# A spectral-mixing and GeGLU kernel on one core: soft threshold and half of the gates computed in place in PSUM, a pace for the background work in each stretch, and the inverse transform placed ahead of the last products

## The chip, the cores and the metric

The kernel runs on one core of one Trainium2 chip. The metric is the device time of one execution in microseconds (us), lower being better; the number compared is the median of several executions. The engines are named as the profile names them: PE (TensorE's matmuls), PEld (TensorE's weight loads), DVE (VectorE), ACT (ScalarE), POOL (GpSimd), SP (SyncE, which here only starts DMAs).

## What is computed

Everything works on x, 8192 rows of 448 numbers. Its layer norm goes into a spectral filter (branch A) and into a gated feed-forward network (branch B):

```python
D, F, NB, BS = 448, 1792, 4, 112
def A(x):                                   # x after the layer norm
    Xf = rfft2(x, axes=(1, 2))              # along the 8192 rows
    z = Xf.reshape(B, H, Wf, NB, BS)
    hr = relu(zr @ w1[0] - zi @ w1[1] + b1[0]); hi = relu(zi @ w1[0] + zr @ w1[1] + b1[1])
    or_ = hr @ w2[0] - hi @ w2[1] + b2[0];      oi_ = hi @ w2[0] + hr @ w2[1] + b2[1]
    or_ = sign(or_) * max(abs(or_) - 0.01, 0);  oi_ = sign(oi_) * max(abs(oi_) - 0.01, 0)
    return irfft2(or_ + 1j * oi_)
def Bf(x):
    return (gelu(x @ w_gate) * (x @ w_up)) @ w_down
xn = layernorm(x)
out = x + A(xn) * silu(Bf(xn))
```

The line with `sign` is the soft threshold. The factor `silu(Bf(xn))` is called the gate here. (Cut from the reference, which is evaluated in float32.)

## The kernel before

**Numbers in pairs.** TensorE is fed with float16. Each float32 operand is cut into a float16 head and a float16 rest (`hi`, `lo`), and a product becomes three matmuls: head by head, head by rest, rest by head. So most values that TensorE reads pass through one cast (ACT) and one subtraction (DVE or POOL).

**Branch B is the foreground.** Its products fill TensorE almost throughout. The 8192 rows come in 16 chunks of 512, and the hidden width of 1792 is done in two passes: pass 0 takes the first eight blocks of 128, pass 1 the last six. In `chunk`, the up and gate products of a chunk are built from seven smaller products per pair of blocks (`unit`: `a1` to `a7`), and the product with `w_down` is built from seven as well (`down2`, `prod2`). Between these, ACT computes the gelu, DVE multiplies by the up half (`glu`), and `sums` forms the sums and the head and rest pairs that the seven down products need. These sums are the tensors named `wt` in pass 1 and `u`, `gl` in pass 0; the pairs end in `h`, `left` and, again, `wt`.

`down2` holds two PSUM banks, x and y, out of the ring `BD`. A bank collects one product, DVE adds it to a running total in SBUF (`add2`, the tensor `left`), and the bank is used for the next product. Pass 0 stores the totals to HBM (`prt`); pass 1 loads them again (`pt_loads`), adds, and `ended2` turns the total into the gate: ACT takes tanh, DVE computes (tanh + 1) * total. The gate goes to HBM (`gsp`) or, once the inverse transform has begun (`state["direct"]`), straight into the output through `gate`.

**Branch A is the background.** It is woven between the products of the foreground in three phases. Phase 1 (`chunk1`, 16 chunks) normalizes x and does the first step of the transform (`stage1`); beside it the weights of branch B are scaled and split (`gu_comb`, `maxima`, `largest`, tensors `wst`, `wo`, `mxr`). Phase 2 (`phase2`, `group`) has 16 groups of frequencies by four channel blocks, 64 in all: second step of the transform, first layer with its relu (`layer1`), second layer, soft threshold, first step of the inverse transform (`stage3`). Phase 3 (`tiles3`, `gate_bank`) is the last step of the inverse transform, the multiplication by the gate and the sum with x, and writes the output. PSUM for the background comes out of `BF`; `BF` and `BD` share four banks (`Banks`), and a background request leaves one free unless the foreground already holds two.

**The soft threshold of a group.** The second layer's sum stands in a PSUM bank `b`. ACT writes relu(s * b - t) into the SBUF tensor `o`. A second piece goes into the SBUF tensor `va`: relu(-s * b - t) from ACT, or min(b + t', 0) from DVE, whichever engine is free earlier in the plan. The bank is given back. Then `o` becomes the difference of the two (DVE, or POOL where only a subtraction is left), and `halves` turns `o` into head and rest: ACT writes the head into `va`, DVE the rest.

**The plan.** No scheduler of the chip decides the order. The Python code itself keeps a clock for each engine (`Pace`) with estimated durations, and emits each instruction when the plan says that its inputs are there; the emitted order of each engine is then fixed. Semaphores hold back whatever is early on the chip. What steers it:

- `STEPS`, a table whose rows start at a planned time and hold: an allowance for DMA landings in us, how far an engine may be booked ahead before a background instruction is held, a factor on the planned durations, and a handicap for POOL. `Either` (the engine `B`) sends a subtraction or sum to DVE or to POOL, whichever ends earlier in the plan after the handicap; a negative one favours POOL.
- Due times of the background: phase 1 starts a chunk every 34 us (`DT`), phase 2 spreads its groups until `END2`, phase 3 its tiles until `END3`.
- `calm`, which lets a background instruction wait in the plan while foreground work is due on the engine.

All instructions are recorded by one helper, so every instruction of the profile stands on line 288 (290 in the changed kernel, which is two lines longer there). They are told apart by their tensors. In the order, a name like `bd_66` is one of the four shared PSUM banks (66 to 69), `by` and `bx` are the foreground's own banks, `th` the gate, `g` the gate loaded from HBM, `ms`, `fc`, `rowc` columns of factors.

The edited places are `STEPS` (line 43), `note` (150), `last_half` (1780), `ended2` (1797), the soft threshold in `group` (2311 to 2335), `END3` (2368), `phase2`, `phase3` (2462) and `first` (2785).

Of the kernel before, what the change touches and what calls it, by code (L numbers as in the profile page):

```python
# [11 lines left out]
F32 = mybir.dt.float32  # L12
# [10 lines left out]
NG = 16  # L23
CH = 4
# [18 lines left out]
STEPS = ((0, 2.75, 0.05, 0.97, 0.0), (15, 2.75, 0.05, 0.97, 0.0), (25, 2.75, 0.05, 1.0, 0.3), (35, 2.75, 0.05, 1.0, 0.3), (45, 2.75, 0.05, 1.07, 0.0), (55, 2.75, 0.05, 1.07, 0.0), (65, 2.75, 0.05, 0.97, 0.0), (75, 2.75, 0.05, 0.97, 0.0), (87, 2.75, 0.15, 1.01, 0.0), (100, 2.75, 0.15, 1.01, 0.0), (125, 2.5, 0.15, 1.04, 0.0), (150, 2.5, 0.15, 1.04, 0.0), (175, 2.5, 0.15, 1.04, 0.0), (200, 2.5, 0.15, 1.04, 0.0), (225, 3.0, 0.15, 0.98, 0.0), (250, 2.75, 0.05, 1.0, 0.0), (275, 2.75, 0.05, 1.0, 0.0), (300, 2.75, 0.05, 1.0, 0.0), (325, 2.5, 0.05, 1.02, 0.0), (350, 2.5, 0.05, 1.02, 0.0), (375, 2.5, 0.05, 1.04, -0.3), (400, 2.5, 0.05, 1.04, -0.3), (425, 2.5, 0.05, 1.04, -0.3), (450, 2.5, 0.05, 1.04, -0.3), (475, 2.5, 0.05, 1.04, -0.3), (500, 2.5, 0.05, 1.04, -0.3), (525, 2.5, 0.05, 1.04, -0.3), (550, 2.5, 0.05, 1.04, -0.3), (575, 3.5, 0.05, 1.0, 0.0), (600, 3.5, 0.05, 1.0, 0.0), (625, 3.5, 0.05, 1.04, 0.0), (650, 3.5, 0.05, 1.04, 0.0), (675, 3.5, 0.05, 1.04, 0.0), (700, 3.5, 0.05, 1.04, 0.0), (725, 2.75, 0.05, 1.0, 0.0), (750, 2.75, 0.05, 1.0, 0.0), (775, 3.0, 0.05, 1.0, -0.3), (800, 3.0, 0.05, 1.0, -0.3), (825, 3.0, 0.05, 1.0, -0.5), (850, 3.0, 0.05, 1.0, -0.5), (875, 3.0, 0.05, 1.0, -0.5), (900, 3.0, 0.05, 1.0, -0.5), (925, 2.75, 0.05, 1.06, 0.0), (950, 2.75, 0.05, 1.06, 0.0), (975, 2.75, 0.05, 1.06, 0.0), (1000, 2.75, 0.05, 1.06, 0.0), (1025, 2.75, 0.05, 1.06, 0.0), (1050, 2.75, 0.05, 1.06, 0.0), (1075, 2.75, 0.05, 1.06, 0.1), (1100, 2.75, 0.05, 1.06, 0.1), (1125, 2.75, 0.05, 1.02, 0.0), (1150, 2.75, 0.05, 1.02, 0.0), (1175, 1.75, 0.05, 1.025, 0.0), (1200, 1.75, 0.05, 1.025, 0.0), (1225, 1.75, 0.05, 1.055, 0.0), (1250, 1.75, 0.05, 1.055, 0.0), (1275, 1.75, 0.05, 1.025, -0.2), (1300, 1.75, 0.05, 1.025, -0.2), (1325, 1.75, 0.05, 1.025, -0.2), (1350, 1.75, 0.05, 1.025, -0.2), (1375, 1.75, 0.05, 1.025, -0.4), (1400, 1.75, 0.05, 1.025, -0.4), (1425, 2.25, 0.1, 1.025, -0.4), (1450, 2.25, 0.1, 1.025, -0.4), (1475, 2.25, 0.1, 1.025, -0.4), (1500, 2.25, 0.1, 1.025, -0.4), (1525, 2.25, 0.1, 1.025, -0.4), (1550, 2.25, 0.1, 1.025, -0.4), (1575, 1.75, 0.1, 1.025, -0.4), (1600, 1.75, 0.1, 1.025, -0.4), (1625, 1.75, 0.1, 1.025, -0.4), (1650, 1.75, 0.1, 1.025, -0.4), (1675, 2.75, 0.05, 0.94, 0.1), (1700, 2.75, 0.05, 0.94, 0.1), (1725, 2.75, 0.05, 0.94, 0.4))  # L43
# [15 lines left out]
class Pace:  # L59
# [496 lines left out]
def afno_geglu_kernel(ctx, tc, x, gu, raw, wd, mlp, b1, b2, c_m, c_mt, c_small, c_rows, out):  # L556
# [1222 lines left out]
    def last_half(i, qq, e, tf, a):  # L1779
# [13 lines left out]
        V.tensor_tensor(th, th, x4, op=ALU.add)  # L1793
        yield
        Q.dma_start(blk(ov[:, CH * i:CH * i + CH, :], *qq)[:, v], th)

    def ended2(p, i, qq, b, R, earlier=None):
# [19 lines left out]
        if i < NG - 1:  # L1817
            yield
            V.scalar_tensor_tensor(th, th, 1.0, q, op0=ALU.add, op1=ALU.mult)
            PT.put(q)  # L1820
            yield
            if i >= state["direct"]:
                yield from gate(i, qq, th)
                Q.dma_start(blk(ov[:, CH * i:CH * i + CH, :], *qq), th)
                TH.put(tf)
                return
            Q.dma_start(blk(chunk_of(gsp, i), *qq), th)
            TH.put(tf)
            EV["gn", i] = EV.get(("gn", i), 0) + 1
            if EV["gn", i] == 4:  # L1830
                done("gsp", i)
            return
# [8 lines left out]
        V.tensor_tensor(th, th, x4, op=ALU.add)  # L1841
# [407 lines left out]
    def group(g, n):  # L2249
# [579 lines left out]
```

## Time and profile before

| | before |
|---|---|
| median of 3 runs | 1739.8 us (1739.71 to 1740.24) |
| the profiled execution's own time | 1737.31 us |
| its span, first to last instruction | 1735.5 us |
| granted TensorE clock | 0.999 |
| PE busy | 1709.6 us of the span, 15654 matmuls |
| DVE, ACT, POOL busy | 1404.9, 1097.0, 937.6 us |
| bytes moved by DMA | 316.63 MB, 182 GB/s over the span |

How to read it. The profiled execution took 1737.31 us; 1735.5 us of that lie between its first and its last instruction, and the remaining 1.8 us around them. It is 2.5 us below the median of the three timed runs, so a gain is worked out against the profiled execution and then taken from the median. PE is busy 99% of the span. That figure counts a matmul as busy from its start to its modelled end, and consecutive ones overlap, so what can be gained without taking products away is only the time in which PE stands still, before, between and after the products. The idle column of the other engines is of interest only where PE waits for them.

### The profile page before, as it was taken

The page shows a single profiled execution, that of the slowest core. Times are in us where ns is not written, and L with a number is a line of the kernel's source. Part 1 is how long each engine was busy: PE and PEld are TensorE (multiplying, and loading weights), DVE is VectorE, ACT ScalarE, POOL GpSimd, SP SyncE. Part 2 cuts the span into 40 slices and gives each one's busy share as a digit, 9 for nine tenths or more (in the row PEclk, how much of TensorE's full clock was granted, in tenths as well). Part 3 has the DMA queues.
Part 4 walks back from the last instruction along what each step waited for, and adds up shares of the span by engine and source line. Part 5 has one row for each costly group of instructions (what it writes and reads, how often), then busy time and mean ns, then how long its engine had stood idle before and what let it go on. Part 6 is the DMA issues. An engine that isn't in the chain of part 4 may idle for free.

```text
span 1735.5 us, 40997 instructions
## 1 busy us (share of the span) xinstructions
PE 1709.6 (99%) x15654; PEld 1434.6 (83%) x15654; DVE 1404.9 (81%) x2438; ACT 1097.0 (63%) x2240; POOL 937.6 (54%) x1291
## 2 busy tenths in 40 slices
PE   9999999999999999999999999999999999999997
PEld 4447677766777999998989999999999999889886
DVE  8999888878885778778777788888888787687787
ACT  6767666757675556678776667666766676333333
POOL 3467666667565574457566454355445454344442
PEclk9999999999999999999999999999999999999999
DMA  7448987878858543254346865544556455999987
GB/s 265 149 135 252 270 254 221 288 206 229 237 163 242 149 124 74 60 127 106 92 111 185 210 163 131 120 120 104 131 139 145 113 134 113 293 287 306 303 288 257
DMA packets 438310, 316.63 MB, mean 182 GB/s; under 512 B 305793, under 2 KB 409601, under 8 KB 436321
## 3 DMA queue, kind: packets, MB, share of 16 engines
q1 hardware_dynamic: 437824, 313.99, 64.6%
q8 instruction: 122, 2.00, 0.5%
q14 instruction: 76, 0.61, 0.1%
q10 hardware_dynamic: 288, 0.03, 0.0%
HBM read 137.93 MB, written 108.25 MB: 142 GB/s over the span
## 4 chain that ended last, share of the span: by engine, by line
PE 44%; DVE 3%; POOL 2%; ACT 1%; issue 1%; SPq 0%; DMA 0%; DVEq 0%; ACTq 0%; POOLq 0%
PE bd L288 19%; PE bx L288 14%; PE by L288 11%; DVE wt L288 1%; DVE th L288 0%; POOL wn L288 0%; POOL h L288 0%; DVE va L288 0%; POOL wt L288 0%; DVE h L288 0%; SPq L288 0%; DVE g L288 0%; ACT h L288 0%; DVE o L288 0%; DVE t L288 0%
## 5 line engine op out<-in xcount | busy, mean ns | idle before, releaser
L288 PEld LDWEIGHTS <-wt 128*128 128x128 f16 x9142 | 884.6, 98 | 160.3 <-issue 9.5
L288 PE MATMUL bx<-xta,wt 128*128 128x256 f16 (+1 forms) x2819 | 354.7, 275 | 2.2 <-ACT by L288 1.3
L288 PEld LDWEIGHTS <-h 128*128 128x128 f16 x2711 | 259.6, 98 | 76.3 <-POOL h L288 1.1
L288 PE MATMUL by<-xtb,wt 128*128 128x256 f16 x2080 | 255.2, 273 | 0.6 <-DVE by L288 0.6
L288 PE MATMUL bd<-dw,h 128*128 128x448 f16 (+1 forms) x1536 | 241.3, 306 | 0.4 <-DVE ysb L288 0.4
L288 POOL TENSOR_TENSOR wt<-wt 128x256 f32<-128x256 f32 x133 | 107.2, 806 | 158.8 <-DVE wt L288 151.5
L288 PE MATMUL bx<-xtb,wt 128*128 128x256 f16 x1248 | 153.3, 273 | 0.0
L288 PE MATMUL by<-xta,wt 128*128 128x256 f16 (+1 forms) x899 | 123.9, 282 | 0.7 <-DVE u L288 0.5
L288 DVE TENSOR_TENSOR by<-bx,u 128x512 f32<-128x512 f32 x104 | 72.2, 695 | 40.4 <-PE bx L288 34.8
L288 ACT ACTIVATE u<-by,fc 128x512 f32<-128x512 f32 (+1 forms) x118 | 73.4, 635 | 49.1 <-PE by L288 47.4
L288 PE MATMUL bx<-left,wt 128*128 128x256 f16 x816 | 99.9, 273 | 1.0 <-ACT by L288 1.0
L288 PE MATMUL bd<-dw,wt 128*128 128x224 f16 (+1 forms) x816 | 97.9, 264 | 1.4 <-DVE left L288 1.4
L288 POOL TENSOR_TENSOR t<-h 112x256 f32<-112x256 f32 (+1 forms) x34 | 26.0, 765 | 125.8 <-ACT h L288 104.9
L288 ACT COPY u<-by 128x512 f32<-128x512 f32 x104 | 60.7, 584 | 49.2 <-PE by L288 49.1
L288 ACT CAST h<-wt 128x512 f16<-128x512 f32 (+1 forms) x128 | 68.4, 535 | 34.0 <-DVE wt L288 28.9
L288 DVE SCALAR_TENSOR_TENSOR left<-bd,ms,left 128x448 f32<-128x448 f32 x96 | 64.3, 680 | 27.1 <-PE bd L288 26.6
L288 DVE TENSOR_TENSOR v<-bx,u 128x512 f32<-128x512 f32 x104 | 71.2, 685 | 16.6 <-PE bx L288 15.9
L288 POOL TENSOR_TENSOR h<-wt,h 128x256 f16<-128x256 f32 (+1 forms) x65 | 71.4, 1106 | 15.5 <-ACT h L288 15.4
L288 PE MATMUL bd<-w2t,wn 113*128 113x112 f16 (+1 forms) x1152 | 78.3, 212 | 0.9 <-DVE bd L288 0.6
L288 ACT COPY by<-bx 128x512 f32<-128x512 f32 x104 | 60.0, 577 | 24.8 <-PE bx L288 24.3
L288 PE MATMUL bd<-wt,h 128*128 128x224 f16 x603 | 72.9, 259 | 0.6 <-POOL h L288 0.5
L288 PEld LDWEIGHTS <-wn 113*128 113x128 f16 (+1 forms) x1152 | 69.3, 97 | 4.1 <-issue 1.2
(280 smaller groups left out, 3801.8 us busy)
## 6 DMA issues: line engine op xcount, KB each, us to landing
xts<-sx SPq DMA_DIRECT2D x32, 480.0 KB, 4.1
x<-in_x SPq DMA_DIRECT2D x17, 896.0 KB, 6.9
t<-ysb SPq DMA_DIRECT2D x64, 224.0 KB, 3.8
prt<-th SPq DMA_DIRECT2D x64, 224.0 KB, 3.3
vt<-va SPq DMA_DIRECT2D x256, 56.0 KB, 2.1
left<-prt SPq DMA_DIRECT2D x64, 224.0 KB, 3.8
u<-t SPq DMA_DIRECT2D x32, 448.0 KB, 6.0
x<-in_x SPq DMA_DIRECT2D x32, 448.0 KB, 6.4
```

What stands on the lines that cost most here:

```text
L288: return self.pace.issue(self.name, kind, out, ins, lambda: fn(out, *args, **kw))
```

## The change

Five edits, and no product is added or taken away; both kernels have 15654 matmuls.

1. **Soft threshold in place.** The tensor `o` is given back as soon as the second layer is summed. The second piece goes into `va` as before (ACT or DVE). The first piece overwrites the PSUM bank itself (ACT), DVE forms the difference in the bank, and `halves` reads head and rest from the bank. The bank is given back after that instead of after the two relus. POOL no longer takes part.
2. **Half of the gates in place.** For the two quarter tiles of a pass 1 chunk that end in a `BD` bank, the running total is added into the bank rather than the bank into the total; tanh and the product read the bank; the bank is given back after the product instead of after the sum. The slot of the total (`PT`) is given back earlier. What follows is moved into a helper, `gated`, unchanged.
3. **A sixth column in `STEPS`, and new values in the others.** The new column multiplies the spacing of the background's due times in all three phases, which are now accumulated step by step. Among the other columns the handicap of POOL changes most: it is -0.5 over most of the second half of the table.
4. **`END3` goes from 1730 to 1716,** and the tiles of phase 3 are spread until 2 us before it.
5. **The last sums with x** (`last_half`, `ended2`) may go to POOL as well as to DVE.

`note` also drops an older PE read of the same extent from the plan's record, which leaves the latest in force and changes no time in it.

```diff
-STEPS = ((0, 2.75, 0.05, 0.97, 0.0), (15, 2.75, 0.05, 0.97, 0.0),
...
+STEPS = ((0, 2.75, 0.05, 1.0, 0.0, 1.0), (15, 2.75, 0.05, 1.0, 0.0, 1.0),
...
@@ note
+        elif e == "PE":
+            was[:] = [x for x in was if x[4] != e or x[2] or x[0] != lo or x[1] != hi]
@@ last_half, and the same in the last chunk's part of ended2
-        V.tensor_tensor(th, th, x4, op=ALU.add)
+        B.tensor_add(th, th, x4)
@@ ended2
+        if R is BD and p == 1 and i < NG - 1:
+            v, q = part(b, 128, 2, DH), EV["ptb", i, qq]
+            V.scalar_tensor_tensor(v, v, cB[1], q, op0=ALU.mult, op1=ALU.add)
+            PT.put(q)
+            yield
+            tf = yield from TH.get()
+            th = tf.rearrange("p (a d) -> p a d", a=2)
+            S.activation(th, v, AF.Tanh)
+            yield
+            V.scalar_tensor_tensor(th, th, 1.0, v, op0=ALU.add, op1=ALU.mult)
+            BD.put(b)
+            yield
+            yield from gated(i, qq, tf, th)
+            return
@@ group
+        P2["o"].put(o_)
         va = yield from P2["va"].get()
-        r = o_, va.rearrange("p s c -> p (s c)").bitcast(F32)
+        r = va.rearrange("p s c -> p (s c)").bitcast(F32)
         pv = part(b, 128, D)
-        yield from calm("ACT")
-        S.activation(r[0], pv, AF.Relu, bias=ms[:, 23:24], scale=ms[:, 20:21])
         both = pace.free["ACT"] < pace.free["DVE"]
         if both:
             yield from calm("ACT")
-            S.activation(r[1], pv, AF.Relu, bias=ms[:, 23:24], scale=ms[:, 32:33])
+            S.activation(r, pv, AF.Relu, bias=ms[:, 23:24], scale=ms[:, 32:33])
         else:
             yield from calm("DVE")
-            V.tensor_scalar(r[1], pv, ms[:, 33:34], 0.0, op0=ALU.add, op1=ALU.min)
-        BF.put(b)
-        yield
-        if both:
-            yield from B.calm("tensor_sub", r[0], r[0], r[1])
-        else:
-            yield from calm("DVE")
-            V.scalar_tensor_tensor(r[0], r[1], ms[:, 20:21], r[0], op0=ALU.mult, op1=ALU.add)
-        yield
-        yield from halves(o_, va, D)
-        P2["o"].put(o_)
+            V.tensor_scalar(r, pv, ms[:, 33:34], 0.0, op0=ALU.add, op1=ALU.min)
+            yield
+            yield from calm("ACT")
+        S.activation(pv, pv, AF.Relu, bias=ms[:, 23:24], scale=ms[:, 20:21])
+        yield
+        yield from calm("DVE")
+        if both:
+            V.tensor_tensor(pv, pv, r, op=ALU.subtract)
+        else:
+            V.scalar_tensor_tensor(pv, r, ms[:, 20:21], pv, op0=ALU.mult, op1=ALU.add)
+        yield
+        yield from halves(pv, va, D)
+        BF.put(b)
@@ due times
-    END1, END2, END3 = T1 + NG * DT + 12.0, 1450.0, 1730.0
+    END1, END2, END3 = T1 + NG * DT + 12.0, 1450.0, 1716.0
@@ phase2
-                at += (END2 - at) / left * (0.94 if state["chunk"][0] == 0 else 1.0)
+                at += (END2 - at) / left * (0.94 if state["chunk"][0] == 0 else 1.0) * pace.step(pace.now)[5]
@@ phase3
-            yield t0 + 10.0 + k * dt
+            yield at
+            at += (END3 - 2.0 - at) / (n3 - k) * pace.step(pace.now)[5]
@@ first
-            yield T1 + (c - PL) * DT
+            yield at
+            at += DT * pace.step(pace.now)[5]
```

Since the plan decides the order, the diff alone doesn't show what moves. Three places follow, as the built programs have them.

**DVE, phase 2, at the first running total of pass 1 that is kept from a `by` bank.** The rows are DVE's queue up to that sum (`left<-by`); `o` and `va` are the soft threshold's tensors, `h_14235` and `h_14226` the first layer's. Before:

```order
L288 TENSOR_SCALAR va<-bd_67,ms 128x448
L288 TENSOR_TENSOR zs<-t,zs 112x256
L288 TENSOR_TENSOR wt_82<-wt_83,wt_82 128x512
L288 SCALAR_TENSOR_TENSOR wt_83<-v_14128,fc,wt_83 128x512
L288 SCALAR_TENSOR_TENSOR o<-va,ms,o 128x448
L288 SCALAR_TENSOR_TENSOR z<-bd_69,z 112x512
L288 SCALAR_TENSOR_TENSOR t<-bd_69,t 112x256
L288 SCALAR_TENSOR_TENSOR left<-bd_66,ms,left 128x448
L288 TENSOR_TENSOR wt_83<-wt_83 128x256
L288 SCALAR_TENSOR_TENSOR va<-va,o 128x448
L288 TENSOR_TENSOR h_14235<-bd_67,h_14235 112x256
L288 SCALAR_TENSOR_TENSOR left<-by,ms,left 128x448
```

The same place now:

```order
L290 TENSOR_SCALAR va<-bd_66,ms 128x448
L290 TENSOR_TENSOR wt_82<-wt_83,wt_82 128x512
L290 TENSOR_TENSOR h_14226<-bd_67,h_14226 112x256
L290 SCALAR_TENSOR_TENSOR bd_66<-va,ms,bd_66 128x448
L290 TENSOR_TENSOR t<-h_14226 112x256
L290 SCALAR_TENSOR_TENSOR wt_83<-v_14210,fc,wt_83 128x512
L290 SCALAR_TENSOR_TENSOR va<-va,bd_66 128x448
L290 SCALAR_TENSOR_TENSOR left<-bd_69,ms,left 128x448
L290 SCALAR_TENSOR_TENSOR u<-u,bd_68 128x4x112
L290 TENSOR_TENSOR wn_8358<-t,wn_8358 112x256
L290 SCALAR_TENSOR_TENSOR left<-by,ms,left 128x448
```

The threshold's two combinations read and write the bank `bd_66` in place of `o`, the sum of `wt_83` with itself has left DVE's queue at this place, and the first layer's sum stands ahead of the threshold rather than behind it.

**DVE, phase 1, the rows ahead of the reduction `mxr`, which PE waits for in `largest`.** `wst`, `rowc` and `wo` belong to the splitting of the weights, `gl`, `v` and `u` to the foreground. Before:

```order
L288 TENSOR_TENSOR by<-bx,u_3269 128x512
L288 TENSOR_REDUCE fm<-wmx 128x1
L288 TENSOR_TENSOR wst<-wst 128x128
L288 TENSOR_TENSOR fx<-fm 128x2
L288 SCALAR_TENSOR_TENSOR wst<-wst,rowc 128x128
L288 SCALAR_TENSOR_TENSOR gl<-v_3256,fc,gl 128x256 x2
L288 TENSOR_REDUCE mxr<-bd_68 2x1
```

The same reduction now:

```order
L290 SCALAR_TENSOR_TENSOR wo<-wo,rowc,wst 128x128
L290 TENSOR_TENSOR by<-bx,u_3386 128x512
L290 SCALAR_TENSOR_TENSOR gl<-v_3371,fc,gl 128x512
L290 TENSOR_REDUCE fm<-wmx 128x1
L290 SCALAR_TENSOR_TENSOR u_3433<-by,fc,u_3433 128x512
L290 TENSOR_TENSOR fx<-fm 128x2
L290 TENSOR_TENSOR h<-gl,h 128x2x256
L290 SCALAR_TENSOR_TENSOR ysb<-bd_66,ysb 128x2x224
L290 TENSOR_REDUCE mxr<-bd_69 2x1
```

No step of the weights' splitting stands between `fx` and `mxr` any more; one sum of the foreground and one eviction from PSUM do.

**PE, the end of the program.** `u` by `mt` are tiles of the inverse transform, all others products of the last chunk. Repeated rows and weight loads are left out. Before:

```order
L288 MATMUL bd_68<-wt_80,h 128x224
...
L288 MATMUL bx<-dw_84,h 128x224
...
L288 MATMUL bx<-wt_80,h 128x224
...
L288 MATMUL bd_66<-u_24554,mt 128x448
...
L288 MATMUL bd_69<-u_24325,mt 128x448
...
L288 MATMUL bd_67<-u_24554,mt 128x448
...
L288 MATMUL bd_66<-u_24606,mt 128x448
...
L288 MATMUL bd_69<-u_24606,mt 128x448
...
L288 MATMUL bd_67<-u_24503,mt 128x448
...
L288 MATMUL bd_66<-u_24503,mt 128x448
...
L2825 UNCONDITIONAL_BRANCH
```

Now:

```order
L290 MATMUL bd_69<-u_24548,mt 128x448
...
L290 MATMUL bd_66<-dw_84,wt_82 128x224
...
L290 MATMUL bd_66<-wt_79,h 128x224
...
L290 MATMUL bd_67<-wt_76,h 128x224
...
L290 MATMUL bd_66<-wt_80,h 128x224
...
L290 MATMUL bx<-wt_80,h 128x224
L2848 UNCONDITIONAL_BRANCH
```

The seven tiles (21 matmuls) that stood behind the last product now all stand ahead of it. The last of them, shown in the first row, is followed by 54 matmuls of products, and none of the inverse transform is left behind them.

More of the change, by code (lines that the diff above doesn't have):

```diff
@@ L1792, in last_half, with gated @@
         yield
-        V.tensor_tensor(th, th, x4, op=ALU.add)
+        B.tensor_add(th, th, x4)
         yield
         Q.dma_start(blk(ov[:, CH * i:CH * i + CH, :], *qq)[:, v], th)
+    def gated(i, qq, tf, th):
+        if i >= state["direct"]:
+            yield from gate(i, qq, th)
+            Q.dma_start(blk(ov[:, CH * i:CH * i + CH, :], *qq), th)
+            TH.put(tf)
+            return
+        Q.dma_start(blk(chunk_of(gsp, i), *qq), th)
+        TH.put(tf)
+        EV["gn", i] = EV.get(("gn", i), 0) + 1
+        if EV["gn", i] == 4:
+            done("gsp", i)
     def ended2(p, i, qq, b, R, earlier=None):
@@ L1802, in ended2 @@
             pace.spawn(gate_bank(i, qq))
+        if R is BD and p == 1 and i < NG - 1:
[11 more added lines that the diff above has]
+            yield from gated(i, qq, tf, th)
+            return
         yield from add2(p, i, qq, b)
@@ L1821, in ended2 @@
             yield
[L1822 to L1831, printed above, removed]
+            yield from gated(i, qq, tf, th)
             return
@@ L1840, in ended2 @@
         yield
-        V.tensor_tensor(th, th, x4, op=ALU.add)
+        B.tensor_add(th, th, x4)
         PT.put(q)
@@ L2450, in phase3 @@
         t0 = pace.now
-        dt = (END3 - t0 - 12.0) / n3
+        at = t0 + 10.0
         pace.spawn(load3(order[0]))
@@ L2795, in first @@
         done("phase", 1)
+        at = T1
         for c in range(PL, NG + PL):
             done("phase", c - 1)
-            yield T1 + (c - PL) * DT
+            yield at
+            at += DT * pace.step(pace.now)[5]
             if c > PL + 1:
```

2 lines of the change are left out of this document (1 added, 1 removed).

## Prediction

> **What bounds the kernel now.** The page comes first: its span and the busy time of the engines.
>
> ```profile
> span 1735.5 us, 40997 instructions
> PE 1709.6 (99%) x15654; PEld 1434.6 (83%) x15654; DVE 1404.9 (81%) x2438; ACT 1097.0 (63%) x2240; POOL 937.6 (54%) x1291
> ```
>
> PE is the bound, and the change leaves its 15654 matmuls alone. All that can be gained is 1735.5 - 1709.6 = 25.9 us in which PE stands. The busy time by stretches says where they lie; each row has the stretch, its length, and then the busy us of each engine.
>
> ```profile
> 0.00:25.00 25.00, 21.73 (x128) 11.95 (x129) 17.79 (x38) 12.49 (x29) 7.07 (x21) 1.00 0.88 317
> 25.00:600.00 575.00, 568.25 (x4109) 398.81 (x4108) 485.02 (x905) 388.96 (x777) 366.10 (x626) 1.00 0.74 217
> 600.00:1460.00 860.00, 855.08 (x8995) 789.31 (x8994) 691.96 (x1183) 591.94 (x1255) 460.44 (x535) 1.00 0.50 124
> 1460.00:1700.00 240.00, 239.96 (x2217) 214.51 (x2216) 182.49 (x265) 92.20 (x161) 95.58 (x101) 1.00 0.94 289
> 1700.00:1721.70 21.70, 20.36 (x191) 18.02 (x189) 18.94 (x32) 7.85 (x14) 8.01 (x8) 1.00 0.73 258
> 1721.70:1735.50 13.80, 4.18 (x24) 2.00 (x21) 8.69 (x18) 3.54 (x7) 0.44 (x1) 0.82 0.54 195
> ```
>
> PE's idle time is the length less the second number: 3.3 us in the start, then 6.7, 4.9 and 0.0 (11.7 from 25 to 1700 us), 1.3 in the last products, 9.6 in the last row. In the middle DVE is the busiest engine beside PE (485 of 575 us, 692 of 860). PE's own waits, longest first in total (us, times, longest):
>
> ```profile
> PE bx L288 <- ACT by L288: 2.3, 3, 1.0
> PE bd L288 <- DVE mxr L288: 2.2, 2, 1.8
> ...
> PE bd L288 <- DVE u L288: 1.1, 1, 1.1
> PE bd L288 <- POOL h L288: 0.5, 1, 0.5
> ```
>
> These are few and single waits, not a steady loss. The end is the largest piece, so its timeline comes next (start, length), with the DMA view's landing times of the last outputs.
>
> ```profile
> 1721.46 0.45 PE L288 MATMUL bx<-wt,h 128*128 128x224 f16 x3
> 1721.74 4.13 PE L288 MATMUL bd<-u,mt 128*128 128x448 f16 x21
> 1721.95 0.45 DVE L288 SCALAR_TENSOR_TENSOR left<-bx,ms,left 128x224 f32<-128x224 f32 x1 [0.18 <-PE bx L288]
> 1724.88 0.63 DVE L288 TENSOR_TENSOR th<-th,s 128x448 f32<-128x448 f32 x1 [0.46 <-ACT s L288]
> 1725.32 0.66 ACT L288 ACTIVATE th<-left 128x224 f32<-128x224 f32 x2
> 1727.52 0.38 DVE L288 TENSOR_TENSOR th<-th,s 128x224 f32<-128x224 f32 x1
> 1731.80 0.36 SPq L288 DMA_DIRECT2D out<-g  x1
> out<-g SPq DMA_DIRECT2D x4, 448.0 KB, 3.1
> out<-th SPq DMA_DIRECT2D x2, 112.0 KB, 1.8
> ```
>
> The last product is done at 1721.91. Then PE works off seven tiles of the inverse transform (21 matmuls, 4.13 us, to 1725.87), and all that depends on them, whole tiles through ACT and DVE, runs for another 5.9 us until the last output is issued at 1731.80; with 3.1 us to land, 0.6 remain to the end of the span.
>
> **The inverse transform ahead of the last products.** The 4.13 us of tile matmuls are not saved; they stand earlier, and PE's last matmul stays where it is if nothing else changes. What follows it becomes shorter. In the new order the last matmul is that of the last half tile. Its sum on DVE (0.45) is queued behind a whole tile's product (0.63, of which about 0.45 is left by then), then Silu (0.33 of the 0.66 for two), then the product with s (0.38): 1.6 us after the last matmul. The sums with x are on POOL now. One row gives a whole tile there, the other the nearest size to a half:
>
> ```profile
> L288 POOL TENSOR_TENSOR th<-th,x 128x448 f32<-128x448 f32 x5 | 6.1, 1212 | 25.2 <-DVE th L288 25.2
> L288 POOL TENSOR_TENSOR wt<-wt 128x256 f32<-128x256 f32 x133 | 107.2, 806 | 158.8 <-DVE wt L288 151.5 <-PE by L288 1.9
> ```
>
> A whole sum (1.21) starts when the whole product is done (0.45) and the two halves follow at 0.8 each, which ends at 3.3. Then 1.8 to land and 0.6 to the end: 5.7 us in place of 9.6, a gain of 3.9. If nothing queues on POOL the tail is 0.45 + 0.33 + 0.38 + 0.8 + 1.8 + 0.6 and some 0.5 of handovers, 4.9; if one more whole sum and its handover stand ahead of the halves, 7.5. So the gain lies between 2.1 and 4.7. Left on DVE, the halves would cost 0.4 each and the tail no more than this; sending them to POOL costs up to 0.8.
>
> The tiles now stand between the products of the last chunk, whose handovers through DVE and POOL make PE wait 1.3 us in the row 1700 to 1721.7. Each tile is 3 matmuls of 4.13 / 21, 0.6 us of cover. I take half of it, 0.7; the bounds are 0, where the tiles' own evictions queue ahead, and 1.3.
>
> **The reduction `mxr`.** Its longest wait, in order of time:
>
> ```profile
> 272.21 3.42 DVE L288 SCALAR_TENSOR_TENSOR wst<-wst,rowc 128x128 f32<-128x128 f32 x1
> 272.24 0.86 POOL L288 TENSOR_TENSOR wst<-wst 64x128 f32<-64x128 f32 x2
> 273.61 1.88 POOL L288 TENSOR_TENSOR xs<-x,xs 128x896 f16<-128x896 f32 x1
> 276.88 0.17 PE L288 MATMUL bd<-ident,mxr 2*128 2x2 bf16 x1 [1.81 <-DVE mxr L288]
> ```
>
> A DVE instruction of 128 columns took 3.42 us: it stood from 272.21 to 275.63 while POOL worked one instruction after another until 275.49. It reads two tensors from SBUF. Its queue stood behind it, `mxr` with it, and PE waited 1.81. In the new order this form of step no longer stands between `fx` and `mxr`, and I count the 1.8 as gained; what stands there reads PSUM or is foreground. The bounds are 0 (a like block elsewhere in the queue) and 2.2, all waits for `mxr`.
>
> The Trainium skill, "SBUF — State Buffer", section Who interferes with whom, says that a DVE instruction with two SBUF inputs contends with a GpSimd instruction that reads SBUF, that whichever holds the shared port pair keeps it for the whole instruction, and that one with at most one SBUF input does not contend. The trace agrees on who is held, but the hold ran through several POOL instructions, not one; by the page alone the loss here would have ended with the first (at most 0.86), PE's wait would not have come about, and the sum below would be 6.9 in place of 8.7.
>
> **The soft threshold and the gates in PSUM.** The same kind of block, twice in phase 2:
>
> ```profile
> 817.53 1.63 DVE L288 SCALAR_TENSOR_TENSOR va<-va,o 128x448 f16<-128x448 f16 x1
> 1015.58 2.40 DVE L288 SCALAR_TENSOR_TENSOR va<-va,o 128x448 f16<-128x448 f16 x1
> 1018.35 0.56 ACT L288 ACTIVATE h<-bd,b1s,ms 112x256 f32<-112x256 f32 x1 [3.05 <-DVE h L288]
> 1021.38 0.81 PE L288 MATMUL bx<-left,wt 128*128 128x256 f16 x6 [0.99 <-ACT by L288]
> ```
>
> The threshold's last step, from two SBUF tensors, was held 2.40 us the second time; the first layer's sum on DVE stood behind it, ACT waited 3.05 for that, and the foreground's copy `by` behind it on ACT came 0.99 too late for PE. What the forms cost in the mean (count, busy us, mean ns):
>
> ```profile
> L288 DVE SCALAR_TENSOR_TENSOR va<-va,o 128x448 f16<-128x448 f16 x64 | 49.1, 768 | 3.8 <-ACT va L288 3.4
> L288 DVE SCALAR_TENSOR_TENSOR u<-u,bd 128x448 f16<-128x448 f16 x65 | 39.7, 612 | 3.2 <-ACT u L288 3.2
> L288 DVE SCALAR_TENSOR_TENSOR o<-va,ms,o 128x448 f32<-128x448 f32 x49 | 38.2, 780 | 0.2
> L288 DVE SCALAR_TENSOR_TENSOR left<-by,ms,left 128x448 f32<-128x448 f32 x16 | 10.8, 677 | 0.4
> L288 DVE TENSOR_SCALAR va<-bd,ms 128x448 f32<-128x448 f32 x49 | 33.5, 683 | 48.2 <-ACT o L288 47.9 <-DMA left<-prt 0.2
> L288 DVE TENSOR_TENSOR wt<-wt 128x256 f32<-128x256 f32 x59 | 30.8, 523 | 3.5 <-POOL wt L288 2.4
> L288 DVE TENSOR_TENSOR wt<-wt,wt 128x512 f16<-128x512 f32 x42 | 35.4, 844 | 1.3 <-ACT wt L288 1.1
> L288 POOL TENSOR_TENSOR wt<-wt,wt 128x512 f16<-128x512 f32 x22 | 27.3, 1239 | 10.6 <-ACT wt L288 10.4
> ```
>
> The same step with one input in PSUM (`u<-u,bd`) takes 612 ns against 768: 64 times 0.156 is 10 us of DVE. The combination falls from 780 to the 677 of `left<-by`, and from 49 to 28 times: 38.2 to 19.0. DVE now also makes 36 subtractions in the bank, some 24 us at 0.68, where it made 14 in SBUF, some 11 at the combination's 0.78. The second piece goes from 49 to 28 times 0.683 on DVE, 14 less, and to ACT. From 59 `wt` sums 11 stay on DVE (25 less), from 42 `wt,wt` 15 (23 less); POOL gets them at 806 and 1239 ns. In all DVE loses some 80 us of the 902 that the last four rows of the stretches add up to, 9%. None of that is on the path by itself. It counts through waits, and 1.0 + 1.1 of them (the `by` wait above, and the one wait of `bd` for `u`, which came 4 us after the block of 1.63) go with such blocks: I take 2.1 as gained, between 0 and the 4.9 that PE stands from 600 to 1460 in all. The other waits of the middle I leave as they are: a new plan will move them, and I have no row that says which way.
>
> The sum against the profiled execution: 3.9 + 0.7 + 1.8 + 2.1 = 8.5, with the smaller `mxr` wait (2.2 - 1.8, and 0.4 halved) 8.7. So 1737.31 - 8.7 = 1728.6 in a profile. The profiled execution lies 2.5 us below the median, so the median comes to 1739.8 - 8.7 = 1731.1, forecast as 1731. About 0.2%, 3.5 us, is what can be told from no change.
>
> **Rivals.** *Only the end moves* (0.22). The blocks of DVE go where the new plan puts them, and the middle's 11.7 us stay. Then 3.9 + 0.7 count: 1739.8 - 4.6 = 1735.2. For it: POOL gets more work, and each POOL instruction is one that can hold DVE. Against it: in the new order some 250 steps of DVE stop reading two SBUF tensors or leave DVE.
>
> *The banks run short* (0.13). A group gives its bank back after three more steps, two on DVE (0.68 and 0.61) and one on ACT between them, some 2 us in all, and the gates hold theirs for two; the four banks are shared with the running totals. If 16 of the 64 groups make PE wait 0.5 us more, 8 us are gone: 1739.1, no change. For it: the order is fixed by a plan that knows only estimates. Against it: PE's waits show none of any size for a bank.
>
> *POOL becomes late for the products with `w_down`* (0.07, slower). The sums of a chunk's last pair of blocks go from DVE to POOL, where one costs 0.28 to 0.4 us more, and their pairs `h` are what the last w_down products wait for; today that wait is 0.5, once. Should the chain outrun PE's cover in each of pass 1's 16 chunks by 0.85, that is 13.6 us: 1739.8 - 8.7 + 13.6 = 1744.7. It decides from the point where the added POOL time of a chunk's last pair, below 1 us by these rows, exceeds what PE still has to do. The Trainium skill, "GPSIMD Engine Reference", section Engine selection, advises against this move: two-input elementwise work on GpSimd is given as about 2 times slower. The rows here say 1.5 times (806 to 523, 1239 to 844).
>
> **How the numbers follow.** The forecast has 0.55, its own range 1726 to 1735; 0.03 is left for a plan that removes nearly all waits, 3.9 + 0.7 + 11.7 = 16.3 us, 1723.5. The range reaches from there to the third case's upper side: 1723 to 1739.5. Faster by over 0.2% (below 1736.3): the forecast nearly whole, three quarters of the first rival, and the 0.03, with part of the second's spread: 0.77. Within 0.2%: 0.16. Slower: 0.07.
>
> **What would show it.** In the changed profile the last row of PE should be products, the idle time after it 5 to 7 us, and the waits from 1700 on below 1 us. PE's longest wait for `mxr` should be below 0.5. `va<-va,bd` should take about 0.61 and never over 1 us, DVE's busy time should fall by some 80 us and POOL's rise by more. It is wrong if PE's idle time from 25 to 1700 us is not below 11.7, if POOL `h` or a bank leads the list of PE's waits, or if the tail is still over 8 us.

## The result, and the profile after

| | before | after |
|---|---|---|
| median, run side by side | 1740.02 us (1739.71 to 1742.28, 4 runs) | 1727.99 us (1727.14 to 1729.31, 4 runs) |
| ratio | | 0.9929, 95% interval 0.9912 to 0.9946 |
| the profiled execution's own time | 1737.31 us | 1729.31 us |
| its span | 1735.5 us | 1727.2 us |
| PE idle in the span | 25.9 us | 18.1 us |

The change made the kernel faster by 12.0 us at the median, 0.7%; the forecast was 1731. The profiled executions differ by only 8.0: that of before is 2.7 below its kernel's median, that of after is the longest of its four. The page of the changed kernel, span and busy times:

```profile
span 1727.2 us, 41012 instructions
PE 1709.1 (99%) x15654; PEld 1435.5 (83%) x15654; DVE 1345.0 (78%) x2317; ACT 1103.3 (64%) x2242; POOL 1014.2 (59%) x1410
```

PE does the same matmuls in the same time (1709.6 before). DVE is relieved by 59.9 us, POOL gets 76.6 more. Busy time by stretches (stretch, length, then PE, PEld, DVE, ACT and POOL, the granted clock, DMA):

```profile
25.00:600.00 575.00, 569.57 (x4113) 400.04 (x4112) 476.74 (x897) 393.17 (x779) 370.06 (x629) 1.00 0.74 216
600.00:1460.00 860.00, 858.45 (x9042) 793.40 (x9040) 659.48 (x1120) 597.16 (x1258) 491.03 (x610) 1.00 0.51 126
1460.00:1700.00 240.00, 240.00 (x2209) 214.00 (x2207) 172.83 (x240) 90.53 (x160) 127.12 (x133) 1.00 0.95 296
1700.00:1721.70 21.70, 19.41 (x172) 16.02 (x169) 16.88 (x24) 9.68 (x17) 16.92 (x17) 1.00 0.63 218
1721.70:1727.20 5.50, 0.00 (x0) 0.00 (x0) 1.17 (x2) 0.20 (x1) 1.97 (x3) 0.66 0.32 105
```

PE's idle time is 5.4, 1.6 and 0.0 us in the first three rows (6.7, 4.9 and 0.0 before): 7.0 in the middle in place of 11.7. In the fourth row 1.2 us are waits of the last products (1.3 before) and the rest lies behind the last matmul. The largest waits of PE (us, times, longest):

```profile
PE bx L290 <- ACT by L290: 2.6, 2, 1.9
PE bx L290 <- DVE v L290: 2.2, 2, 1.4
PE bx L290 <- DVE gl L290: 1.5, 1, 1.5
PE bd L290 <- POOL h L290: 1.1, 2, 0.8
...
PE bd L290 <- DVE mxr L290: 0.4, 1, 0.4
```

The waits for `mxr` and `u`, which stood high in the list before, are small now (0.4 and 0.3), but `by` and `v` have waits as long. The end, in order of time (start, length):

```profile
1720.20 0.45 PE L290 MATMUL bx<-wt,h 128*128 128x224 f16 x3
1720.49 0.63 DVE L290 TENSOR_TENSOR th<-th,s 128x448 f32<-128x448 f32 x1
1721.03 0.45 DVE L290 SCALAR_TENSOR_TENSOR left<-bx,ms,left 128x224 f32<-128x224 f32 x1
1721.19 1.13 POOL L290 TENSOR_TENSOR th<-th,x 128x448 f32<-128x448 f32 x1 [0.78 <-DVE th L290]
1721.39 1.48 DVE L290 TENSOR_TENSOR th<-th,s 128x224 f32<-128x224 f32 x2
1722.65 1.35 POOL L290 TENSOR_TENSOR th<-th,x 128x224 f32<-128x224 f32 x2 [0.33 <-DVE th L290]
```

PE's last row is a product now and ends at 1720.65; what follows it, called the tail, takes 6.5 us in place of 9.6. The two half products on DVE need 0.74 each (0.38 before): they start while POOL's whole sum runs.

### The profile page after: what moved, and what is told of

It reads as the page before. It is cut to its first block, busy times and chain, and to the rows that moved or that the text cites. A ratio compares the mean times of both kernels' runs of the same rounds, so it can differ in the third digit from the quotient of the medians.

```text
span 1727.2 us, 41012 instructions
## 1 busy us (share of the span) xinstructions
PE 1709.1 (99%) x15654; PEld 1435.5 (83%) x15654; DVE 1345.0 (78%) x2317; ACT 1103.3 (64%) x2242; POOL 1014.2 (59%) x1410
## 4 chain that ended last, share of the span: by engine, by line
PE 87%; DVE 6%; ACT 2%; DMA 2%; POOL 2%; issue 1%; SPq 0%; POOLq 0%; DVEq 0%; ACTq 0%
PE bd L290 35%; PE bx L290 30%; PE by L290 22%; DMA prt<-th 1%; DVE st L290 1%; ACT wt L290 1%; DVE raws L290 0%; POOL st L290 0%; DVE ysb L290 0%; DVE wt L290 0%; DVE dw L290 0%; DVE left L290 0%; DVE u L290 0%; DMA xta<-xts 0%; DVE h L290 0%
## 5 line engine op out<-in xcount | busy, mean ns | idle before, releaser
L290 POOL TENSOR_TENSOR wt<-wt 128x256 f32<-128x256 f32 x181 | 140.2, 775 | 94.0 <-DVE wt L290 84.7
L290 POOL TENSOR_TENSOR h<-wt,h 128x512 f16<-128x512 f32 (+1 forms) x92 | 96.1, 1058 | 35.9 <-ACT h L290 35.4
L290 POOL CAST zs<-t 112x256 f16<-112x256 f32 (+2 forms) x45 | 21.3, 474 | 123.1 <-DVE t L290 107.9
L290 DVE SCALAR_TENSOR_TENSOR u<-by,fc,u 128x512 f32<-128x512 f32 (+1 forms) x86 | 55.2, 656 | 18.7 <-PE by L290 12.9
```

The lines of the kernel that those rows point to most:

```text
L290: return self.pace.issue(self.name, kind, out, ins, lambda: fn(out, *args, **kw))
```

## The experiments

Twelve kernels were run, each against the kernel before on the same chip (1738.5 to 1739.9 us at the median). The row of the changed kernel is that of the first table, with its own runs of before, so the ratios compare better across rows than the medians. PE's idle time (us) is read from the busy time by stretches; the tail is the span behind PE's last matmul.

| kernel | median us | ratio (95%) | PE idle 25 to 600 | 600 to 1460 | 1460 to 1700 | tail |
|---|---|---|---|---|---|---|
| before (profile) | 1740.0 | 1 | 6.7 | 4.9 | 0.0 | 9.6 |
| after | 1728.0 | 0.9929 (0.9912 to 0.9946) | 5.4 | 1.6 | 0.0 | 6.5 |
| e1, the end alone | 1744.0 | 1.0027 (1.0016 to 1.0038) | 7.6 | 4.9 | 0.0 | 7.3 |
| e2, after without the end | 1732.6 | 0.9961 (0.9948 to 0.9973) | 5.7 | 1.5 | 0.7 | 8.2 |
| e3, after with the old pace | 1747.8 | 1.0049 (1.0037 to 1.0062) | 6.8 | 5.7 | 3.6 | 9.5 |
| e4, the pace alone | 1742.5 | 1.0019 (1.0010 to 1.0028) | 3.8 | 10.8 | 2.7 | 5.8 |
| e5, after with the old threshold | 1753.1 | 1.0082 (1.0067 to 1.0096) | 5.0 | 15.6 | 5.8 | 5.8 |
| e6, after with the old gates | 1736.9 | 0.9988 (0.9979 to 0.9996) | 5.2 | 5.5 | 0.8 | 5.9 |
| e7, after with the last sums on DVE | 1727.5 | 0.9935 (0.9922 to 0.9948) | 5.2 | 1.5 | 0.0 | 5.8 |
| e8, after without POOL's handicaps | 1744.5 | 1.0034 (1.0022 to 1.0046) | 9.2 | 5.9 | 1.2 | 9.7 |
| e9, after, cost factors + 0.005 | 1746.8 | 1.0044 (1.0031 to 1.0057) | 11.4 | 8.3 | 2.8 | 5.8 |
| e10, after, cost factors - 0.005 | 1744.4 | 1.0027 (1.0016 to 1.0037) | 7.8 | 7.8 | 3.0 | 5.8 |
| e11, before, cost factors + 0.005 | 1762.6 | 1.0134 (1.0116 to 1.0151) | 17.8 | 12.7 | 2.5 | 9.3 |
| e12, before, cost factors - 0.005 | 1754.6 | 1.0087 (1.0073 to 1.0101) | 13.3 | 10.8 | 0.0 | 9.2 |

### The end

**e1**, on the kernel before:

```diff
-    END1, END2, END3 = T1 + NG * DT + 12.0, 1450.0, 1730.0
+    END1, END2, END3 = T1 + NG * DT + 12.0, 1450.0, 1716.0
```

> The kernel before with END3 at 1716 and nothing else: the tiles of the inverse transform go ahead of the last products, the old pace and the old steps stay. Theory A (the end is worth its own term, whatever the rest does): the tail after the last matmul falls from 9.6 us to 6 or 7, the middle keeps its idle time, and the time falls by 2.5 to 4 us to 1736 to 1737.5. Theory B (the end pays only with the pace that was set for it): the tiles push back the last products' sums on DVE and POOL, PE waits 2 us or more from 1690 on, and the time stays within 1.5 us of 1740.

By the traces PE's matmuls keep the order of before up to the 14503rd of 15654, at 1597.7 us. The tail falls to 7.3, yet the time rises by 4.8 us. PE's waits and SP's issues near the end:

```profile
PE bd L288 <- DMA mt<-c_mt: 4.9, 2, 4.2
```

```profile
1717.80 0.33 SPq L288 DMA_DIRECT2D g<-gsp  x1
1722.12 0.34 SPq L288 DMA_DIRECT2D out<-g  x1
1722.55 0.39 SPq L288 DMA_DIRECT2D u<-t  x1
1722.99 0.67 SPq L288 DMA_DIRECT2D mt<-c_mt  x1
```

The loads `u` and `mt` for the last tiles stand in SP's queue behind the store of an earlier tile, which SP can issue only when DVE has made its `g`, at 1722.12. `mt` lands 4.3 us after its issue, and the products behind these tiles on PE wait with them. Neither theory had this: A had the tail about right and missed the wait, B had a wait but named other queues and no loss.

The wait is not the whole price. From 1726 to 1732 the granted clock is 0.50, and PE is busy 2.1 us longer with the same matmuls than before (1711.7 against 1709.6). Of the 5.8 us between the two spans, 4.8 are waits of the last products, 2.1 this busy time and 1.2 idle time elsewhere, and the tail gives 2.3 back. In the changed kernel the last `mt` load is issued at 1705.63, ahead of the last two stores of `g`. Of the other runs with `END3` at 1716, e3 and e6 wait for `mt` too, 1.9 and 2.9 us.

**e2**, the changed kernel with the line above set back to 1730:

> The changed kernel with END3 back at 1730. Theory A: the last row of PE is tiles again, the tail goes from 6.5 us back to 9 or 10 and the time rises by 2.5 to 4 us, to 1730.5 to 1732. Theory B: the end's pace factors of 1.06 are set for 1716, so that more tiles pile up behind the products and the time rises by over 5 us, to 1733 or more.

The busy times around the end:

```profile
1700.00:1721.70 21.70, 19.18 (x159) 15.80 (x158) 13.02 (x19) 8.00 (x14) 10.92 (x12) 0.92 0.38 135
1721.70:1730.70 9.00, 0.78 (x6) 0.34 (x4) 5.59 (x9) 1.77 (x4) 3.10 (x3) 0.80 0.31 102
```

It is 4.6 us slower than the changed kernel by the medians and 5.6 by the ratios, more than A allowed. The picture of neither theory came: PE's last row is still a product (`bx<-wt,h`, at 1722.03), with three tiles between the products from 1714 on (one in the changed kernel). The middle up to 1460 is the same within 0.3. The tail is 8.2, 1.7 more, and from 1460 to the last matmul PE waits 2.0 more; one wait of 2.3 for POOL's `h` leads the list there. So `END3` at 1716 is worth some 4 us on this order, about half as tail and half as shorter waits of the last products, and it costs 4.8 on the order of before.

### The pace and the steps, one without the other

**e3** is the changed kernel with the old table:

```diff
-STEPS = ((0, 2.75, 0.05, 1.0, 0.0, 1.0), (15, 2.75, 0.05, 1.0, 0.0, 1.0),
+STEPS = ((0, 2.75, 0.05, 0.97, 0.0, 1.0), (15, 2.75, 0.05, 0.97, 0.0, 1.0),
...
```

**e4** is the kernel before with the new table and the lines that use its sixth column:

```diff
-                at += (END2 - at) / left * (0.94 if state["chunk"][0] == 0 else 1.0)
+                at += (END2 - at) / left * (0.94 if state["chunk"][0] == 0 else 1.0) * pace.step(pace.now)[5]
...
+            at += (END3 - 2.0 - at) / (n3 - k) * pace.step(pace.now)[5]
...
+            at += DT * pace.step(pace.now)[5]
```

> The changed kernel with the old table of paces (its spacing factors all 1): the new steps in PSUM and the new end stay. Theory A (the steps in PSUM remove DVE's blocks and with them PE's waits): PE's idle time from 25 to 1700 us stays near the 7.0 of the changed kernel, at most 8.5, and the time is 1728 to 1730.5. Theory C (the new pace, not the new steps, removed the waits of the middle): the idle time goes back to 11 us or more, and the time is 1732 to 1736.

> The kernel before with the new table of paces and its spacing factors, and nothing else: threshold, gates, last sums and END3 as before. Theory A: PE's idle time from 25 to 1700 us stays near 11.7, the tail near 9.6, and the time within 2 us of 1740. Theory C: the idle time of the middle falls to 7 or 8, the tail stays, and the time is 1734.5 to 1736.5. A third way: the new paces fit the new steps only, and on the old ones PE's idle time in the middle rises over 14, so that the time is above 1742.

Both are slower than before. e3 refutes A: with all the new steps PE's idle time from 25 to 1700 is 16.1, not below 8.5, and the loss is larger than C had it. e4 went the third way, 17.3 us idle.

No theory had e4's tail, which falls to 5.8 with `END3` still at 1730. Its last row of PE:

```profile
1731.95 0.45 PE L288 MATMUL bx<-wt,h 128*128 128x224 f16 x3
```

So the new table can put a product last without the new `END3`. e3, with the new `END3` and the old table, ends on a product as well, but its tail is 9.5: ACT waits 3.76 us there for a store of `th` to land. A product at the end does not make the tail short by itself.

The pair settles one stretch. By the traces PE's matmuls keep the order of before in e3 up to 684 us and that of the changed kernel in e4 up to 681, about where the soft threshold begins; so up to there the table with its spacing alone sets PE's order. Busy times of e3, then of e4:

```profile
25.00:680.00 655.00, 647.68 (x4896) 472.41 (x4896) 546.62 (x1015) 435.69 (x879) 419.85 (x692) 1.00 0.70 201
```

```profile
25.00:680.00 655.00, 651.16 (x4952) 476.36 (x4951) 539.78 (x1007) 446.02 (x896) 428.89 (x710) 1.00 0.70 202
```

PE's idle time in this stretch is 7.3, 8.1 and 7.3 us in the traces with the old order (before, e1, e3) and 5.4, 5.7, 3.8, 5.0, 5.2 and 5.2 in those with the new one (the changed kernel, e2, e4 to e7). So some 2 us of the change are the table's, and this is shown. The wait for `mxr`, which the prediction counted as gained, lies in this stretch. PE's waits from 260 to 290 us, first in e3, then in the changed kernel:

```profile
PE bd L290 <- DVE mxr L290: 1.8, 1, 1.8
PE bd L290 <- DVE fx L290: 0.4, 1, 0.4
```

```profile
PE bx L290 <- DVE v L290: 1.4, 1, 1.4
```

In e4 the wait for `mxr` is gone as well, and 0.5 for `v` stands there. The table decides who waits, and the new steps don't touch it.

### One step undone

**e5** puts the threshold of before back into the changed kernel, **e6** takes out the gates in a `BD` bank, **e8** sets each negative handicap of the table to 0 (one entry of the table is shown; all three edits are cut):

```diff
-        S.activation(pv, pv, AF.Relu, bias=ms[:, 23:24], scale=ms[:, 20:21])
+        S.activation(r[0], pv, AF.Relu, bias=ms[:, 23:24], scale=ms[:, 20:21])
...
-        yield from halves(pv, va, D)
-        BF.put(b)
+        yield from halves(o_, va, D)
+        P2["o"].put(o_)
```

```diff
-        if R is BD and p == 1 and i < NG - 1:
...
-            yield from gated(i, qq, tf, th)
-            return
```

```diff
-(775, 3.0, 0.05, 1.04, -0.5, 1.0),
+(775, 3.0, 0.05, 1.04, 0.0, 1.0),
```

> The changed kernel with the old soft threshold (made in an SBUF buffer, its bank given back after two steps), the rest as changed. Theory A: the 64 last steps of it take some 0.77 us in place of 0.61 again, single ones are held to 1.6 us or more, PE's idle time from 600 to 1460 us rises by 2 to 3.4 from 1.6, and the time by as much, to 1730 to 1731.5. Theory C (the plan decides, not the step): DVE gets the 10 us more to do, but PE's idle time in that stretch changes by less than 1 us, either way, and the time stays within 1.2 us of 1728.

> The changed kernel with the gates in SBUF for all tiles, the rest as changed. Theory A: few of DVE's steps change, PE's idle time from 1150 to 1700 us stays below 1.5, and the time stays within 1 us of 1728. A rival: the gates in PSUM were what kept DVE on time in pass 1, PE's idle time there rises by 2 us or more, and the time is 1730 or more.

> The changed kernel with the negative handicaps of the table (which send sums to POOL) at 0, so that a sum goes to the engine that is done first by the plan. Theory A (DVE's relief counts): some 30 to 60 us go back to DVE, PE's idle time from 600 to 1460 us rises by 1 to 3, and the time to 1729 to 1731. Rival (POOL's instructions hold DVE, so fewer of them are better): DVE's instructions that stand over 0.3 us beyond the shortest of their form lose less time than the 136 us of the changed kernel, and the time falls by 0.5 to 2 us.

Against the changed kernel all three lose far more than the steps' own prices: 25, 9 and 16 us, where the theories on e5 and e8 had at most 3.5 and 3. e6's rival came in its figures (1736.9, and PE's idle time from 1150 to 1700 us is 4.7 in place of 0.0). In e5 the waits are of all kinds:

```profile
PE bd L290 <- POOL h L290: 7.0, 7, 2.0
PE bd L290 <- DVE zs L290: 5.1, 3, 2.5
PE bx L290 <- ACT by L290: 2.5, 5, 0.8
PE bd L290 <- DVE left L290: 2.0, 4, 0.7
```

A threshold step on DVE that is 0.12 us longer in the mean (0.729 against 0.611), 64 times, gives no reason for waits of 7 us for POOL's `h`. What the three have in common is that the plan was laid anew from the first edited instruction on: PE's order leaves that of the changed kernel at 681, 1030 and 316 us. In e8 DVE's work did become lighter per instruction, as its rival said: `h<-wt,h` of 128x512 takes 0.80 us there and 1.01 in the changed kernel. But 77 us more of it is on DVE (1421.9), and the time rose.

**e7** leaves PE's order as it is, for all 15654 matmuls:

```diff
-        B.tensor_add(th, th, x4)
+        V.tensor_tensor(th, th, x4, op=ALU.add)
```

> The changed kernel with the last sums (th plus x) on DVE alone, at both places; PE's order does not change. Theory D (POOL both takes longer over a sum and holds DVE's product th with s, 0.74 each in place of 0.38): the tail falls from 6.5 us to 5 or 5.5, and the time by 1 to 1.5 us. Rival: DVE's queue is full in the tail, six more sums of 0.4 to 0.6 us stand ahead of the last product, and the tail stays at 6.5 or grows to 7.5.

Its end, in order of time:

```profile
1717.28 0.45 PE L290 MATMUL bx<-wt,h 128*128 128x224 f16 x3
...
1719.10 0.92 DVE L290 TENSOR_TENSOR th<-th,x 128x448 f32<-128x448 f32 x2
1719.94 0.38 DVE L290 TENSOR_TENSOR th<-th,s 128x224 f32<-128x224 f32 x1
1720.36 0.39 DVE L290 TENSOR_TENSOR th<-th,x 128x224 f32<-128x224 f32 x1
```

The product with s takes 0.38 again, the last sum ends 3.0 us after the last matmul in place of 3.35, and the tail is 5.8 in place of 6.5. D had the mechanism and up to twice the size. The gain of 0.8 does not stand clear in the times: the two ratios agree within their intervals.

### The same kernels in another order

The last four shift the fourth column of `STEPS` by 0.005, the factor by which the plan lengthens its estimates. No step, end or spacing changes, but the order does: by the traces PE's matmuls leave the order of the unshifted kernel at 30 to 41 us. The line shown is cut.

```diff
-STEPS = ((0, 2.75, 0.05, 1.0, 0.0, 1.0), (15, 2.75, 0.05, 1.0, 0.0, 1.0),
+STEPS = ((0, 2.75, 0.05, 1.005, 0.0, 1.0), (15, 2.75, 0.05, 1.005, 0.0, 1.0),
```

> The changed kernel with each of the table's cost factors 0.005 higher: the same steps, end and paces, but another order of the background work from the first chunks on. Theory M (the change's parts carry the gain, in any order that the table lays): within 2 us of 1728. Theory L (the gain is in one order that was picked out; any other costs, as the parts undone one by one did): PE's idle time from 25 to 1700 us rises from 7 to 12 or more, and the time is 1733 to 1748.

> The changed kernel with each cost factor 0.005 lower. Theory M: within 2 us of 1728. Theory L: PE's idle time from 25 to 1700 us rises to 12 or more, and the time is 1733 to 1748.

> The kernel before with each of its table's cost factors 0.005 higher. Theory M: within 2 us of 1739. Theory L: this order too was one picked out, PE's idle time from 25 to 1700 us rises from 11.7 to 15 or more, and the time is 1743 to 1755. The mean of this run and the next, less the mean of the two on the changed kernel, is what steps, paces and end are worth in an order that nobody picked: 10 to 12 by theory M, 0 to 8 by theory L.

> The kernel before with each cost factor 0.005 lower. Theory M: within 2 us of 1739. Theory L: PE's idle time from 25 to 1700 us rises to 15 or more, and the time is 1743 to 1755.

Busy times of e9, then of e11, in the middle:

```profile
25.00:600.00 575.00, 563.57 (x4059) 393.75 (x4058) 473.73 (x894) 392.00 (x781) 383.16 (x648) 1.00 0.74 216
600.00:1460.00 860.00, 851.72 (x8950) 784.90 (x8948) 657.34 (x1134) 586.09 (x1239) 455.39 (x562) 1.00 0.51 123
```

```profile
25.00:600.00 575.00, 557.17 (x3967) 385.10 (x3965) 474.24 (x882) 387.44 (x770) 363.53 (x633) 1.00 0.74 215
600.00:1460.00 860.00, 847.35 (x8905) 781.03 (x8905) 695.11 (x1182) 582.88 (x1235) 435.38 (x512) 1.00 0.51 123
```

M is refuted four times, and e11 lies above even L's range: a shift of half a per cent in an estimate costs the changed kernel 18.8 and 16.4 us, the kernel before 22.8 and 14.7. Each of the two kernels stands in an order better than the neighbours that were tried. This is why e3, e4, e5, e6 and e8 say little about the part that they undo, once their order has changed: their loss of 9 to 25 us against the changed kernel is as large as that of a new order with nothing undone. L missed in its other half: the mean ratios of the pairs are 1.0110 and 1.0036, and the difference of 0.0075, 13 us, is more than the 0 to 8 that it allowed. The two orders of one kernel lie 2 and 8 us apart, so this 13 is rough. It comes out near the 12 measured, which fits that steps, pace and end together are worth something like it in orders that nobody picked; two orders of each kernel don't show it. Of the parts, the tail is the steady one in these four: 5.8 in both orders of the changed kernel, 9.2 and 9.3 in those of before. Beyond them it goes by the order too: 9.5 in e3 and 9.7 in e8, both with `END3` at 1716.

## Where the prediction was right and where not

The sum was 8.7 us against the profiled execution. By the idle time the profile shows 3.1 (tail) + 0.1 (last products) + 1.3 (25 to 600 us) + 3.4 (600 to 1460) = 7.9, and 8.3 in the span. Three of the terms came out smaller than forecast and one larger, and their errors cancel in part; that much of the hit is luck.

**The tail: 3.9 forecast, 3.1 measured.** The chain to the last sum was worked out as 3.3 us and took 3.35, with one whole sum ahead of the two halves on POOL, as said. What the prediction missed lies behind it: 2.4 to land and end, measured 3.2. That sending the sums to POOL costs up to 0.8 held in size (e7: 0.8), but only 0.3 of it lies in the chain to the last sum and the rest behind it. The prediction did not ask which edit puts the tiles ahead; by e4 the table can do it without the new `END3`.

**The waits of the last products: 0.7 forecast, 0.1 measured.** They went from 1.3 to 1.2 us, where a sign to look for was below 1. One of 0.76 for POOL's `h` remains at 1713, where three such subtractions follow one another on POOL. In e2 15 tile matmuls in place of 21 stand between 1700 us and the like wait, and it is 2.3. That fits a cover over a wait that had grown, but the two orders differ in more than these tiles.

**`mxr`: 1.8 forecast, and this step failed.** It was right that the blocking step no longer stands ahead of `mxr`, whose longest wait is 0.4 now. It failed where it counted PE's wait as gained. DVE and POOL of the changed kernel there:

```profile
273.96 3.42 DVE L290 SCALAR_TENSOR_TENSOR wst<-wst,rowc 128x128 f32<-128x128 f32 x1
277.31 1.49 DVE L290 TENSOR_TENSOR h<-gl,h 128x512 f16<-128x512 f32 x1
278.72 0.68 DVE L290 TENSOR_TENSOR v<-bx,u 128x512 f32<-128x512 f32 x1
```

```profile
272.26 1.67 POOL L290 TENSOR_TENSOR sf<-x 128x192 f32<-128x192 f32 x2
273.89 0.86 POOL L290 TENSOR_TENSOR wst<-wst 64x128 f32<-64x128 f32 x2
274.72 0.66 POOL L290 TENSOR_TENSOR wo<-wst,wo 128x256 f16<-128x256 f32 x1
275.35 1.88 POOL L290 TENSOR_TENSOR xs<-x,xs 128x896 f16<-128x896 f32 x1
```

The same instruction is held for the same 3.42 us behind the same kind of POOL work. `mxr` is no longer behind it; the foreground's `v` is, and PE waits 1.44 for that. This was the lower bound that the prediction named, a like block elsewhere in the queue. What the stretch did gain, 1.3 us, is the table's by e3 and e4. The rows also speak again on the rule of the Trainium skill, "SBUF — State Buffer", Who interferes with whom: whoever issues first has the shared port pair for the whole instruction (the page says it of DVE's two-port modes). Here DVE's instruction ended only after four of POOL's had passed, those of the last three rows.

**The steps in PSUM: 2.1 forecast, 3.4 measured from 600 to 1460, but not shown to be theirs.** The durations of the threshold's steps came as predicted. Groups of the changed kernel (count, busy us, mean ns):

```profile
L290 DVE SCALAR_TENSOR_TENSOR va<-va,bd 128x448 f16<-128x448 f16 x64 | 39.0, 611 | 3.6 <-ACT va L290 3.4
L290 DVE SCALAR_TENSOR_TENSOR bd<-va,ms,bd 128x448 f32<-128x448 f32 x28 | 19.1, 680 | 1.3 <-ACT bd L290 1.1
L290 DVE TENSOR_TENSOR bd<-bd,va 128x448 f32<-128x448 f32 x36 | 22.6, 627 | 9.4 <-ACT bd L290 9.3
L290 DVE TENSOR_TENSOR h<-wt,h 128x512 f16<-128x512 f32 x31 | 31.2, 1005 | 8.4 <-ACT h L290 8.1
```

The threshold's last step takes 0.611 in the mean, 0.622 at most, where single ones had been held to 2.4: with one input in PSUM none of the 64 is held. DVE was relieved by 59.9 us and not by 80; some 5 of the missing 20 are in the row `h<-wt,h` on DVE, which still reads two tensors from SBUF and takes 1.005 beside the busier POOL (0.84 before, 31 times 0.165). That this is what emptied the stretch of waits was only argued. e3 shows that the steps don't do it in every order: under the old pace they leave 5.7 us idle there. What they are worth in one and the same order no run shows.

**The other waits of the middle.** "A new plan will move them, and I have no row that says which way" is the sentence that the runs put in first place. Moving them by a shift of half a per cent cost 15 to 23 us, more than the whole sum. The forecast held because the new order was again a good one, which no row of before could tell. That was luck. The rivals should have had this case, with its price on the slower side: of the nine new orders tried on either kernel (e3 to e6 and e8 to e12) eight were slower than before. None of the prediction's three rivals came: the middle did change (7.0 in place of 11.7), PE's longest waits on `bd` for an eviction that frees a bank are 0.7 (`ysb`) and 0.5 (`left`), and POOL's `h` costs 1.1 us.

**Between 8.3 and 12.0** lie the two executions that were profiled. One piece of it, 1.7 us, can be seen in the trace of the changed kernel and not in that of before (below); the rest is no larger than the spread of executions, in which before ranged from 1737.1 to 1742.3, and no run assigns it.

## What to carry to other kernels

Where a kernel's order is laid by a plan of estimates, an edit re-lays everything behind it, and the time of one edited kernel can say more about the order than about the edit. Shift an estimate by half a per cent in both kernels, look at the spread, and compare parts only as far as PE's order stays (here e7 throughout, e3 and e4 up to 680 us, e1 and e2 up to their last stretch). A blocked instruction that moves is not a blocked instruction gone: look up who stands behind it in the new order before counting its wait as gained. Work put ahead of the last products must have its loads issued ahead of the stores that wait for results on the same queue.

## What the runs showed of the hardware

A wait of PE can cost its length and then some. In the profiled execution of the changed kernel PE waited 1.89 us for `by` at 153.5; busy times in steps of 2 us, the granted clock being the third number from the end:

```profile
152.00:154.00 2.00, 1.46 (x12) 0.98 (x11) 1.83 (x5) 2.00 (x6) 0.68 (x2) 1.00 0.83 232
154.00:156.00 2.00, 0.65 (x7) 0.58 (x7) 2.00 (x5) 1.95 (x6) 2.00 (x4) 1.00 0.87 224
156.00:158.00 2.00, 2.00 (x14) 1.48 (x12) 1.97 (x5) 1.24 (x3) 2.00 (x4) 0.70 0.94 284
158.00:160.00 2.00, 2.00 (x12) 1.39 (x11) 1.93 (x6) 0.84 (x2) 1.22 (x7) 0.50 1.00 281
160.00:162.00 2.00, 2.00 (x19) 1.76 (x18) 1.94 (x5) 1.10 (x3) 0.00 (x0) 0.95 1.04 374
```

For 3.4 us the clock was half: 0.6 + 1.0 + 0.1 = 1.7 us of work lost, which counts as busy time and in no list of waits. It does not follow each wait. Of the 23 waits over 1.8 us in the 14 traces (up to 1721 us), 11 were followed by such a stretch, and so was one of 1.77 in e10, at 8.0 us. The same wait of 2.54 for `zs` at about 799 us had none in e4 and one in e5; the longest, 3.75 in e12, had none; and one such stretch, in e5 at 1289, came without a wait over 1.2. The Trainium skill, "TensorE: Matmul & The Clock Gate", HAM oscillation — how this bites in real kernels, gives the rule that PE should have no idle gaps above about 3.4 us. Here gaps from 1.77 us on were followed by half the clock, about every second time.
